# Decay attention and two expert layers on one core: the first head pair's scores from fp32 products of q and k as loaded, and the order list made anew

## The chip, the cores and the metric

The program runs on one core of a Trainium2 chip. The metric is device time in microseconds (us); three runs of the kernel before gave 971.85, 974.48 and 971.40, the median is 971.85.

## What is computed

Attention with a decay over 4 x 8 heads of 576 positions and 64 columns, then two layers, each an expansion to 2048 columns, an elementwise function and a contraction to 512, over 2304 tokens.

```python
scores = scale * np.matmul(q, k.transpose(0, 1, 3, 2))
log_f = np.log(np.clip(f, 0.0001, 1.0))
cum = np.cumsum(log_f, axis=-1)
decay = cum[:, :, :, None] - cum[:, :, None, :]
scores = np.where(causal, -1000000000.0, scores + decay)
attn = np.exp(scores - np.max(scores, axis=-1, keepdims=True))
attn = attn / (np.sum(attn, axis=-1, keepdims=True) + 1e-09)
out = np.matmul(attn, v)
```

The row term of the decay drops out with the row maximum, so only the column term, -8 times the running sum of log f, is added to the unscaled scores.

## The kernel before

**Attention.** The 32 heads are 16 pairs; the two heads of a pair lie in partitions 0 to 63 and 64 to 127. A pair has nine score blocks (S0 to S8): the last 64 rows of both heads together (576 columns, cut into 320 and 256, through q with the other head's half zeroed, `qd`), and for each of four further row blocks one block a head, of 512, 384, 256 and 128 columns. The two heads of such a row block are products on the two row halves of the array. A score is the sum of three fp32r products of high and low parts: `hi` (ScalarE, L415) casts k and q to the high part, `lo` (L419, VectorE or GpSimd) subtracts, `diag` (L422) makes qdh and qdl. Per block, in `tasks_of_pair`: S on TensorE (L460, L469), M the sum with the decay and mask and its row minimum on VectorE (L509), E the exponential on ScalarE (L521), T the transposes on TensorE (L533), C their copy out of PSUM on ScalarE or VectorE (L381, L383); per pair the value products V (L570, fp32 on column halves), the copy O of their sum, and R1 to R6 for the row sums.

**The decay.** f is loaded into 32 partitions (`ft`), clipped (L655), its logarithm taken (L706) and summed along the row by a scan (L658). From pair 1 on a pair's decay comes back from DRAM, broadcast over the partitions (`cb`, stored by L712, loaded by L227 and L230), and GpSimd masks it (L238). The first pair does not wait for that way: the sums are split into a high and a low part (L665, L671), four DMAs carry these rows to partitions 0, 1, 64 and 65 of `ct` (L233), and a fourth product with ones (`one`, `oned`) adds them into the scores.

**The layers.** `gemm_in` (h, L758) and `gemm_out` (a, L852, L854; in the filling time L839) are again three products of parts each. Two of the five token chunks of layer 1 go, for four of 16 weight groups, between the attention's products. Weights come as 64-bit floats and are taken apart by ScalarE, VectorE and GpSimd (`convert`, `split`).

**The order.** All is written by hand as tasks with an engine, a duration, dependences and buffers; `plan` goes through them like a list scheduler and writes each engine's instructions in the order of its own clock. `NUDGE` moves the keys of given tasks. Each engine runs its list in order and waits where an operand isn't there. TensorE begins with 26 warming products on zeros (`warm`, L652).

Of the kernel before, what the change touches and what calls it, by code (L numbers as in the profile page):

```python
# [7 lines left out]
F32 = mybir.dt.float32  # L8
# [10 lines left out]
def kernel(ctx, tc, qT, kT, v, f, w_in1, w_out1, w_in2, w_out2, a, b, out):  # L19
# [21 lines left out]
    W_EARLY = 4  # L41
    W_MID = 5
# [99 lines left out]
    def w_load(m, g, half):  # L142
# [43 lines left out]
    for n in range(2):  # L191
        POOL.memset(vt[n][0:QB, NC - 1, :], 0.0)
        POOL.memset(rt_[n][:], 0.0)
    one, oned = [ap1.tile([P, P], F32R, name=f"one{x}") for x in range(2)]
    half = ap1.tile([P, 2], F32, name="half")
    POOL.memset(half[:], 0.0)
    POOL.memset(oned[:].bitcast(F32), 0.0)
    for j in range(2):
        pp = slice(j * QB, (j + 1) * QB)
        POOL.memset(half[pp, j:j + 1], 1.0)  # L200
        POOL.memset(oned[j * QB:j * QB + 2, pp].bitcast(F32), 1.0)
    POOL.memset(one[:].bitcast(F32), 1.0)
    POOL.memset(ct[0][:].bitcast(F32), 0.0)
# [20 lines left out]
    def load_c(pr):  # L224
        if pr:
            t = cb[pr % 2]
            SP.dma_start(t[:, 0:2, :].rearrange("p j s -> p (j s)"), cd[pr:pr + 1, :].broadcast_to([P, 2 * S]))  # L227
        for j in range(2):
            if pr:
                SP.dma_start(t[j * QB:(j + 1) * QB, 2, :], cd[pr:pr + 1, j * S:(j + 1) * S].broadcast_to([QB, S]))  # L230
                continue
            for x in range(2):
                SP.dma_start(ct[0][j * QB + x:j * QB + x + 1, :].bitcast(F32), ft[j:j + 1, 2 + x, :].bitcast(F32))  # L233
# [38 lines left out]
    MOVE, LAND = 1.4, 1.4  # L272
# [118 lines left out]
    def tasks_of_pair(pr):  # L391
# [777 lines left out]
```

## Time and profile before

| what | us |
|---|---|
| median of three runs | 971.85 |
| span of the profiled execution | 969.2 |
| TensorE busy | 956.1 (99%) |
| VectorE busy | 707.6 (73%) |
| ScalarE busy | 629.7 (65%) |
| GpSimd busy | 436.0 (45%) |

For the profiled execution the page gives the span from the first to the last instruction, and no other time. TensorE's products are pipelined, so a busy share of 99% says that something was under way, and not that it ran at its peak. The attention takes about the first 215 us, the first layer lasts to about 570, the second to the end. PEld is the loading of weights into the array, SPq the issuing of DMAs by SyncE.

### The profile page before, as it was taken

How to read it: one execution, taken by the hardware profiler on the slowest of the kernel's cores; microseconds unless marked ns; L12 is line 12 of the kernel's file. 1: busy time of each engine (PE TensorE's matmuls, PEld its weight loads, DVE VectorE, ACT ScalarE, POOL GpSimd, SP SyncE). 2: the span in 40 equal slices, each digit the busy share in tenths (PEclk: the TensorE clock that was granted, in tenths of full speed). 3: DMA queues.
4: the chain of work that ended last, by engine and by line, in shares of the span. 5: the costliest groups of instructions: out<-in, count | busy, mean ns of one | idle time of the engine just before them, and what ended most of it. 6: DMA issues, size and time to landing. Idle time of an engine off the chain costs nothing.

```text
span 969.2 us, 15465 instructions
## 1 busy us (share of the span) xinstructions
PE 956.1 (99%) x5124; PEld 783.1 (81%) x5124; DVE 707.6 (73%) x1391; ACT 629.7 (65%) x1327; POOL 436.0 (45%) x490
## 2 busy tenths in 40 slices
PE   8999999999999999999999999999999999999998
PEld 5667777778888888888888998888888888888887
DVE  7898889963878967867755779776666766766565
ACT  6999888875654434334334579777677677766675
POOL 3766745636455422322221235444445454444444
PEclk9999999999999999999999999999999999999999
DMA  7897798756553565755742650010101100010010
GB/s 231 256 287 236 230 284 283 246 174 197 189 192 110 163 209 161 238 174 158 244 131 88 196 168 7 1 44 0 44 12 33 44 1 23 0 44 1 1 44 23
DMA packets 66656, 125.14 MB, mean 129 GB/s; under 512 B 10048, under 2 KB 20944, under 8 KB 66576
## 3 DMA queue, kind: packets, MB, share of 16 engines
q1 hardware_dynamic: 66576, 124.16, 40.0%
q8 instruction: 40, 0.66, 0.3%
q14 instruction: 40, 0.33, 0.1%
HBM read 94.61 MB, written 29.51 MB: 128 GB/s over the span
## 4 chain that ended last, share of the span: by engine, by line
PE 80%; DVE 2%; ACT 1%; issue 0%; POOL 0%; ACTq 0%
PE h L758 38%; PE a L854 20%; PE a L852 17%; PE T L533 1%; PE O L570 1%; PE a L839 1%; PE S L469 1%; DVE wd L113 1%; DVE wd L107 0%; DVE wd L101 0%; PE S L460 0%; ACT wh L127 0%; ACT t L782 0%; DVE t L786 0%; POOL wl L131 0%
## 5 line engine op out<-in xcount | busy, mean ns | idle before, releaser
L772 POOL TENSOR_TENSOR gl<-t,gh 128x512 fp32r<-128x512 f32 (+1 forms) x160 | 196.3, 1228 | 278.7 <-ACT gh L768 202.2
L758 PE MATMUL h<-xh,wl 128*128 128x512 f32 (+1 forms) x640 | 236.9, 370 | 0.2 <-POOL wl L131 0.2
L758 PE MATMUL h<-xl,wh 128*128 128x512 f32 (+1 forms) x640 | 235.5, 368 | 0.0
L758 PE MATMUL h<-xh,wh 128*128 128x512 f32 (+1 forms) x640 | 235.5, 368 | 0.0
L768 ACT CAST gh<-t 128x512 fp32r<-128x512 f32 (+1 forms) x160 | 93.0, 582 | 117.1 <-PE a L854 47.2
L803 POOL TENSOR_TENSOR t<-t,t 128x512 f32<-128x512 f32 (+1 forms) x80 | 94.5, 1181 | 129.5 <-ACT t L796 121.2
L758 PEld LDWEIGHTS h<-xh,wl 128*128 128x128 f32 x640 | 120.6, 188 | 20.9 <-POOL wl L131 0.6
L758 PEld LDWEIGHTS h<-xh,wh 128*128 128x128 f32 x640 | 120.6, 188 | 20.0
L758 PEld LDWEIGHTS h<-xl,wh 128*128 128x128 f32 x640 | 120.7, 189 | 19.8
L854 PE MATMUL a<-wh,gl 128*128 128x512 f32 x288 | 112.2, 389 | 0.0
L854 PE MATMUL a<-wl,gh 128*128 128x512 f32 x288 | 112.2, 389 | 0.0
L854 PE MATMUL a<-wh,gh 128*128 128x512 f32 x288 | 112.0, 389 | 0.0
L852 PE MATMUL a<-gh,wl 128*128 128x512 f32 (+1 forms) x288 | 105.3, 366 | 0.0
L852 PE MATMUL a<-gl,wh 128*128 128x512 f32 (+1 forms) x288 | 105.3, 365 | 0.0
L852 PE MATMUL a<-gh,wh 128*128 128x512 f32 (+1 forms) x288 | 105.2, 365 | 0.0
L782 ACT ACTIVATE t<-t 128x512 f32<-128x512 f32 (+1 forms) x80 | 47.1, 589 | 75.8 <-DVE t L777 75.6
L777 DVE TENSOR_SCALAR t<-h 128x512 f32<-128x512 f32 (+1 forms) x80 | 50.8, 635 | 60.2 <-PE h L758 59.7
L821 DVE SCALAR_TENSOR_TENSOR t<-t,na,h 128x512 f32<-128x512 f32 (+1 forms) x80 | 55.3, 691 | 53.3 <-ACT h L817 52.4
L521 ACT ACTIVATE P<-P,nm 128x384 f32<-128x384 f32 (+3 forms) x144 | 84.1, 586 | 15.6 <-DVE nm L509 14.6
L807 DVE TENSOR_TENSOR t<-h,t 128x512 f32<-128x512 f32 (+1 forms) x80 | 51.0, 637 | 55.4 <-ACT t L799 55.1
L238 POOL TENSOR_SCALAR_AFFINE_SELECT cb<-cb 128x128 f32<-128x128 f32 (+1 forms) x150 | 56.2, 387 | 62.9 <-DVE nm L509 47.4
L793 ACT ACTIVATE t<-h,ab 128x512 f32<-128x512 f32 (+1 forms) x80 | 51.8, 649 | 43.5 <-PE h L758 43.5
(121 smaller groups left out, 1883.6 us busy)
## 6 DMA issues: line engine op xcount, KB each, us to landing
raw<-in_moe_w_in_dram SPq DMA_DIRECT2D x32, 512.0 KB, 3.7
raw<-in_moe_w_out_dram SPq DMA_DIRECT2D x32, 512.0 KB, 4.2
xr<-xd SPq DMA_DIRECT2D x48, 256.0 KB, 3.9
wfd<-wd SPq DMA_DIRECT2D x42, 256.0 KB, 4.2
wf<-wfd SPq DMA_DIRECT2D x42, 256.0 KB, 2.6
cb<-cd SPq DMA_DIRECT2D x15, 576.0 KB, 9.4
ks<-in_k_dram SPq DMA_DIRECT2D x16, 288.0 KB, 4.7
qs<-in_q_dram SPq DMA_DIRECT2D x16, 288.0 KB, 4.7
```

What stands on the lines that cost most here:

```text
L238: POOL.affine_select(out=t, in_=t, compare_op=ALU.is_ge, fill=-BIG, base=0, pattern=[[-1, n]], channel_multiplier=1,)
L521: ACT.activation(p, p, AF.Exp, scale=-1.0, bias=nm[pr][:, pos:pos + 1], accum_out=ls[pr][:, COL[pos]:COL[pos] + 1])
L758: PE.matmul(hps[g], ww[:, kk * P:(kk + 1) * P], xx[kk], start=(kk == 0 and y == 0), stop=(kk == KD - 1 and y == 2))
L768: ACT.copy(gt[g][0], mid[g][0])
L772: eng.tensor_tensor(out=lo, in0=mid.pop(g)[0], in1=hi.bitcast(F32), op=ALU.subtract)
L777: DVE.tensor_scalar(out=c, in0=hps[g], scalar1=-1.0, scalar2=1.0, op0=ALU.max, op1=ALU.min)
L793: ACT.activation(mid[g]["w"], hps[g], AF.Abs, scale=ab[:, 0:1])
L803: POOL.tensor_tensor(out=vv, in0=vv, in1=mid[g]["w"], op=ALU.add)
L807: DVE.tensor_tensor(out=t, in0=hps[g], in1=t, op=ALU.mult)
L821: DVE.scalar_tensor_tensor(out=t, in0=t, scalar=na[:, 0:1], in1=hps[g], op0=ALU.add, op1=ALU.mult)
L852: PE.matmul(acc[x, d], ww[:, dd], gg, start=st, stop=sp)
L854: PE.matmul(acc[x, d], gg[:, dd], ww[:], start=st, stop=sp)
```

## The change

1. *First pair's scores.* k and q are used as loaded, in plain fp32 (`whole`): one product a block, with `qdw` for the last rows. hi, lo and the two diag of this pair go.
2. *Its decay.* f is loaded twice, into partitions 0 to 31 and 64 to 95 of `fr` (the tile `cb[0]`); the rest is set to 1. The scan runs over all 128 partitions, and a product with a selector (`sel`, `seld`: -8 in the row of a head, zero elsewhere) adds that head's running sum to the scores. The split, the four DMAs, ct, one and oned go.
3. *The opening.* k and q of the first pair are loaded from ScalarE's queue ahead of its table load; GpSimd's fills come in another order; k and q of the second pair are loaded behind the store of the decay. 9 warming products instead of 26.
4. *The order list.* Durations and latencies of the planner are set anew, and NUDGE holds 57 other moves.

The core of the diff (the list of nudges is left out but for a line):

```diff
-    WARM, WARM2 = 12, 14
+    WARM, WARM2 = 9, 0
...
+    qdw = [ap1.tile([P, P], F32, name=f"qdw{n}") for n in range(2)]
...
-    one, oned = [ap1.tile([P, P], F32R, name=f"one{x}") for x in range(2)]
...
+    sel, seld = [ap1.tile([P, P], F32, name=f"sel{x}") for x in range(2)]
...
     def load_pair(pr, x):
...
-            SP.dma_start(t[:], (kT, qT)[x][pr])
+            (SP if pr else ACT).dma_start(t[:], (kT, qT)[x][pr])
...
     def load_c(pr):
...
-            for x in range(2):
-                SP.dma_start(ct[0][j * QB + x:j * QB + x + 1, :].bitcast(F32), ft[j:j + 1, 2 + x, :].bitcast(F32))
...
     NUDGE = [
-        (648, 29, -0.8), (1339, 23, 1.6), (1564, 5, 0.5), (1173, 66, -1.2), (4043, 36, 0.6), (240, 8, -16.0),
...
+        (390, 54, -1.7), (1376, 60, 5.4), (263, 28, 0.9), (453, 2, 3.3), (1491, 27, -3.5), (882, 18, -2.1),
...
         def diag(y, eng):
+            to, src = (qdw[pr % 2], nat[pr, 1]) if whole else ((qdh, qh), (qdl, ql_))[y]
+            src = src[:, S - QB:S]
             ENGINES[eng].tensor_tensor(
-                out=(qdh, qdl)[y][:].rearrange("p (x s) -> p x s", x=2),
-                in0=(qh, ql_)[y][:, S - QB:S].bitcast(F32).unsqueeze(1).to_broadcast([P, 2, QB]),
+                out=to[:].rearrange("p (x s) -> p x s", x=2),
+                in0=(src if whole else src.bitcast(F32)).unsqueeze(1).to_broadcast([P, 2, QB]),
...
-            T("ldc", -99, "sp", [(0.55, 0.05)] * 4, lambda: load_c(pr), ((0, "c"),), ("cb",))
+            T("ldc", -99, "init", 0.0, lambda: None, (), ("cb",))
         ways = ["dvp", "pool"]
         lo_ = [0.68, 1.42]
-        for x, (nm_, tag) in enumerate((("k", "ks"), ("q", "qs"))):
+        if whole:
+            T("qd0", kk + 3, ways, [0.24, 0.4], [lambda e=e: diag(0, e) for e in ways], ("ldq",), ("qdw",))
...
             def s_fn(s=s, b=b, both=both, cuts=cuts):
+                if whole:
+                    k_, q_, cum = nat[pr, 0], nat[pr, 1], fr[:, 1, :]
...
-                        ways = [(qdl[:], kh[:, n0:n1]), (qdh[:], kl_[:, n0:n1]), (qdh[:], kh[:, n0:n1])]
-                        if pr == 0:
-                            ways.append((oned[0:QB + 2], c_[0:QB + 2, n0:n1]))
+                        if whole:
+                            ways = [(qdw[pr % 2][:], k_[:, n0:n1])] + ([] if pr else [(seld[:], cum[:, n0:n1])])
+                        else:
+                            ways = [(qdl[:], kh[:, n0:n1]), (qdh[:], kl_[:, n0:n1]), (qdh[:], kh[:, n0:n1])]
...
-                for x, (qq, kk_) in enumerate(((ql_, kh), (qh, kl_), (qh, kh)) + (((one, c_),) if pr == 0 else ())):
+                if whole:
+                    ways = [(q_[:, qc], k_)] + ([] if pr else [(sel[:], cum)])
+                else:
+                    ways = [(ql_[:, qc], kh), (qh[:, qc], kl_), (qh[:, qc], kh)]
+                for x, (qq, kk_) in enumerate(ways):
                     for jj in range(2):
                         pp = slice(jj * QB, (jj + 1) * QB)
-                        PE.matmul(
-                            ts[jj][:, 0:n], qq[pp, qc] if x < 3 else qq[pp, :], kk_[pp, 0:n], start=(x == 0),
-                            stop=(x == (2 if pr else 3)),
-                        )
+                        PE.matmul(ts[jj][:, 0:n], qq[pp, :], kk_[pp, 0:n], start=(x == 0), stop=(x == len(ways) - 1))
...
-    ft = ap1.tile([NH, 4, S], F32R, tag="PT1", name="ft")
-    zt = ap1.tile([NH, S], F32, tag="PT0", name="zt")
-    SP.dma_start(ft[:, 0, :].bitcast(F32), f.rearrange("b h s -> (b h) s"))
+    fr = cb[0]
+    zt = ap1.tile([P, 1], F32, name="zt")
+    f_ = f.rearrange("b h s -> (b h) s")
+    SP.dma_start(fr[0:NH, 0, :], f_)
+    SP.dma_start(fr[QB:QB + NH, 0, :], f_)
+    load_pair(0, 0)
+    load_pair(0, 1)
+    ACT.preload_act_table_set("natural_log_exp_and_others")
     still = ap1.tile([P, 512], mybir.dt.bfloat16, tag="P", name="still", bufs=PB)
     DVE.memset(still[:], 0.0)
     DVE.memset(zt[:], 0.0)
-    load_pair(0, 0)
-    load_pair(0, 1)
+    DVE.memset(fr[NH:QB, 0, :], 1.0)
+    POOL.memset(fr[QB + NH:P, 0, :], 1.0)
+    POOL.memset(half[:], 0.0)
+    for j in range(2):
+        POOL.memset(half[j * QB:(j + 1) * QB, j:j + 1], 1.0)
+
+    def equal(t, base):
+
+        n = t.shape[1]
+        POOL.affine_select(
+            out=t, in_=t, compare_op=ALU.not_equal, fill=-ROOT, base=base, pattern=[[0, n]], channel_multiplier=1,
+        )
+
+    for t in (seld, sel):
+        POOL.memset(t[:], 0.0)
+        for j in range(2):
+            pp = slice(j * QB, (j + 1) * QB)
+            equal(t[pp, pp if t is seld else slice(0, P)], -j)
...
-    cum = ft[:, 1, :].bitcast(F32)
-
-    def c_hi():
-        ACT.activation(ft[:, 2, :], cum, AF.Copy, scale=-ROOT)
+    cum = fr[:, 1, :]
 
     def c_all():
-        ACT.activation(ft[:, 0, :].bitcast(F32), cum, AF.Copy, scale=-ROOT)
-
-    def c_lo():
-        DVE.scalar_tensor_tensor(
-            out=ft[:, 3, :], in0=cum, scalar=-ROOT, in1=ft[:, 2, :].bitcast(F32), op0=ALU.mult, op1=ALU.subtract
-        )
+        ACT.activation(fr[0:NH, 2, :], cum[0:NH, :], AF.Copy, scale=-ROOT)
...
-    t = task(-99, "act", 0.57, c_hi, (t,))
-    t2 = task(-98, "act", 0.57, c_all, (t,))
-    t = tid[0, "c"] = task(-99, "dve", 0.67, c_lo, (t,))
+    t = tid[0, "c"] = task(-99, "dve", 1.35, lambda x=x: f_scan(cum, x), (t,))
+    t = task(-99, "act", 0.57, c_all, (t,))
```

**TensorE, the first pair's scores, before** (S are score tiles, kh and kl the parts of k, ql, qh, qdl, qdh those of q, ct the decay's rows):

```order
L652 LDWEIGHTS still
L652 MATMUL warm<-still 128x512
L460 MATMUL S_0_224<-kh_115,qdl_124 128x320 [waits DVE_49,Activation_49]
L460 MATMUL S_0_224<-kl_116,qdh_123 128x320
L460 MATMUL S_0_224<-kh_115,qdh_123 128x320
L460 MATMUL S_0_224<-ct_129,one_139 128x320 [waits DMAHW2_49,DMAHW1_49,DMAHW3_49,DMAHW0_49,Pool_49]
L460 MATMUL S_320_229<-kh_115,qdl_124 128x256
L460 MATMUL S_320_229<-kl_116,qdh_123 128x256
L460 MATMUL S_320_229<-kh_115,qdh_123 128x256
L460 MATMUL S_320_229<-ct_129,one_139 128x256
L469 MATMUL S_0_236<-kh_115,ql_120 128x512
```

**and with the change** (ks, qs are k and q as loaded, qdw q with the other half zeroed, cb the tile of the running sums, sel the selectors):

```order
L661 LDWEIGHTS still
L661 MATMUL warm<-still 128x512
L433 MATMUL S_0_191<-ks_129,qdw_111 128x320 [waits DMAHW0_49,Pool_49]
L433 MATMUL S_0_191<-cb_113,sel_123 128x320 [waits DVE_49]
L433 MATMUL S_320_194<-ks_129,qdw_111 128x256
L433 MATMUL S_320_194<-cb_113,sel_123 128x256
L446 MATMUL S_0_202<-ks_129,qs_131 128x512 [waits DMAHW2_49]
L446 MATMUL S_0_203<-ks_129,qs_131 128x512
L446 MATMUL S_0_202<-cb_113,sel_122 128x512
L446 MATMUL S_0_203<-cb_113,sel_122 128x512
```

Three products of parts and one with the rows that DMAs bring have become one of k and q and one with the running sums; the first now waits for a DMA and for GpSimd, the second for VectorE.

**ScalarE, from the logarithm of f to the first exponentials, before** (P are the exponentials' tiles, nm the row minima):

```order
L706 ACTIVATE ft<-ft 32x576 [waits DVE_49]
L665 ACTIVATE ft<-ft 32x576 [waits DVE_49]
L668 ACTIVATE ft<-ft 32x576 [waits Activation_49]
L415 CAST kh_115<-ks_157 128x576 [waits DMAHW1_49]
L415 CAST qh_119<-qs_159 128x576 [waits DMAHW2_49]
L415 CAST kh_117<-ks_179 128x576 [waits DMAHW5_49]
L415 CAST qh_121<-qs_182 128x576 [waits DMAHW6_49]
L521 ACTIVATE P_250,ls_249<-P_250,nm_248 128x576 [waits DVE_49]
L521 ACTIVATE P_257,ls_249<-P_257,nm_248 128x512 [waits DVE_49]
L521 ACTIVATE P_272,ls_249<-P_272,nm_248 128x512 [waits DVE_49]
```

**and with the change**:

```order
L181 DMA ks_129<-in_k_dram 128x576
L181 DMA qs_131<-in_q_dram 128x576
L621 ACT_TABLE_LOAD
L708 ACTIVATE cb_113<-cb_113 128x576 [waits DMAHW3_49,DMAHW1_49,DVE_49]
L674 ACTIVATE cb_113<-cb_113 32x576 [waits DVE_49]
L496 ACTIVATE P_212,ls_211<-P_212,nm_210 128x576 [waits DVE_49]
L380 CAST kh_101<-ks_198 128x576 [waits DMAHW7_49]
L496 ACTIVATE P_225,ls_211<-P_225,nm_210 128x512 [waits DVE_49]
L496 ACTIVATE P_228,ls_211<-P_228,nm_210 128x512 [waits DVE_49]
L346 COPY PT_1_254<-T_0_238 128x8x64 [waits PE_49]
```

The casts of the second pair (kh_117, qh_121 before, kh_101, qh_105 now) have moved from ahead of the first exponential to behind the first and the fourth, and one copy of transposes stands between.

**GpSimd, the end of its fills, with the change** (tri are the masks of the first pair, vt and rt tiles for v and the row sums):

```order
L643 MEMSET tri 128x512 [waits Pool_49]
L644 MEMSET tri_120 128x256
L199 AFFINE_SELECT tri<-tri 128x128 [waits Pool_49]
L199 AFFINE_SELECT tri_120<-tri_120 64x64 [waits Pool_49] x2
L648 MEMSET ident 128x128 [waits Pool_49]
L649 AFFINE_SELECT ident<-ident 128x128 [waits Pool_49]
L654 MEMSET vt_115 64x128
L655 MEMSET rt_117 128x128
L654 MEMSET vt_116 64x128
L655 MEMSET rt_118 128x128
L389 TENSOR_TENSOR qdw_111<-qs_131,half 128x128 [waits DMAHW2_49]
L199 AFFINE_SELECT cb_114<-cb_114 64x64 [waits DMAHW4_49]
```

The last instruction that the first product waits for, qdw, stands behind all fills and ahead of the first mask of pair 1; before, GpSimd had no part in q here, and its fills were followed by that mask at once.

## Rows read from the trace of the kernel before

**Rows 1.** Stretches: length, busy us by engine, granted clock, DMA share, GB/s.

```profile
20.00:40.00 20.00, 19.08 (x158) 13.16 (x156) 18.37 (x63) 19.82 (x63) 13.13 (x23) 1.00 0.83 256
...
300.00:400.00 100.00, 99.79 (x441) 82.33 (x440) 81.44 (x123) 42.00 (x70) 35.08 (x25) 1.00 0.54 169
```

**Rows 2.** Timeline, opening: start, length, engine, line, operation; in brackets idle before.

```profile
2.70 0.45 DVE L655 TENSOR_SCALAR ft<-ft 32x576 f32<-32x576 f32 x1 [0.90 <-DMA ft<-in_f_dram]
...
3.27 0.58 SPq L215 DMA_DIRECT2D ks<-in_k_dram  x1
...
3.90 1.35 DVE L658 TENSOR_TENSOR_SCAN ft<-ft,zt 32x576 f32<-32x576 f32 x1 [0.75 <-ACT ft L706]
...
7.00 2.48 SPq L233 DMA_DIRECT2D ct<-ft  x4
```

**Rows 3.** The same timeline, TensorE.

```profile
1.26 7.56 PE L652 MATMUL warm<-still 128*128 128x512 bf16 x26 [1.26 <-DVE still L643]
...
9.10 0.39 PE L460 MATMUL S<-kh,qdl 128*128 128x320 f32 x1 [0.28 <-ACT qh L415]
...
10.78 0.39 PE L460 MATMUL S<-ct,one 66*128 66x320 f32 x1 [1.00 <-DMA ct<-ft]
```

**Rows 4.** Stretches of 1 us; PEclk is the granted clock.

```profile
11.00:12.00 1.00, 1.00 (x7) 0.83 (x8) 0.32 (x1) 0.00 (x0) 0.00 (x0) 0.86 0.87 255
12.00:13.00 1.00, 1.00 (x8) 0.74 (x6) 0.67 (x4) 0.26 (x1) 0.00 (x0) 0.50 0.73 270
...
15.00:16.00 1.00, 1.00 (x11) 0.83 (x12) 0.82 (x3) 1.00 (x5) 0.00 (x0) 0.94 0.83 212
```

**Rows 5.** Who waited for whom, TensorE, whole run: us, times, longest.

```profile
PE T L533 <- ACT PT L381: 3.2, 6, 0.9
...
PE h L758 <- POOL wl L131: 0.2, 1, 0.2
```

**Rows 6.** The same view, TensorE's weight loads, 20 to 215 us.

```profile
PEld S L469 <- issue: 4.4, 26, 0.2
PEld O L570 <- issue: 3.5, 17, 0.3
...
PEld T L533 <- issue: 2.2, 11, 0.3
```

**Rows 7.** Timeline, GpSimd, opening and one product with half.

```profile
2.25 0.53 POOL L172 TENSOR_SCALAR_AFFINE_SELECT tri<-tri 64x64 f32<-64x64 f32 x2
...
3.71 0.20 POOL L197 MEMSET one<- 128x128 f32 x1
...
4.29 0.34 POOL L201 MEMSET one<- 2x64 f32 x2
...
4.68 0.58 POOL L203 MEMSET ct<- 128x576 f32 x1
...
26.32 0.40 POOL L422 TENSOR_TENSOR qdl<-ql,half 128x128 fp32r<-128x128 f32 x1
```

**Rows 8.** DMA issues of the whole run: KB each, median us to landing.

```profile
ks<-in_k_dram SPq DMA_DIRECT2D x16, 288.0 KB, 4.7
```

**Rows 9.** The chain that ended last: start, length, line, instructions.

```profile
212.29 2.86 PE O L570 x28
...
278.09 2.72 PE h L758 x12
```

**Rows 10.** Timeline, TensorE, row pairs of 512 columns and the next.

```profile
20.80 0.40 PE L469 MATMUL S<-kh,qh 64*128 64x512 f32 x2
...
21.03 0.59 PE L469 MATMUL S<-kh,ql 64*128 64x384 f32 x2
```

**Rows 11.** Timeline, ScalarE, casts and the first exponentials.

```profile
7.66 0.67 ACT L415 CAST kh<-ks 128x576 fp32r<-128x576 f32 x1
...
12.74 0.77 ACT L521 ACTIVATE P<-P,nm 128x576 f32<-128x576 f32 x1 [3.70 <-DVE nm L509]
...
14.31 0.72 ACT L521 ACTIVATE P<-P,nm 128x512 f32<-128x512 f32 x1 [0.70 <-DVE nm L509]
```

More of the change, by code (lines that the diff above doesn't have):

```diff
@@ L41 @@
     W_EARLY = 4
+    WHOLE = 1
     W_MID = 5
@@ L438, in tasks_of_pair @@
               (nm_ + "hi",), (), (tag,))
-        T("qd0", kk + 3, ways, [0.24, 0.4], [lambda e=e: diag(0, e) for e in ways], ("qhi",))
-        T("qd1", kk + 3, ways, [0.24, 0.4], [lambda e=e: diag(1, e) for e in ways], ("qlo",))
+        if not whole:
+            T("qd0", kk + 3, ways, [0.24, 0.4], [lambda e=e: diag(0, e) for e in ways], ("qhi",))
+            T("qd1", kk + 3, ways, [0.24, 0.4], [lambda e=e: diag(1, e) for e in ways], ("qlo",))
         for pos, (b, j) in enumerate(BLOCKS):
@@ L478, in tasks_of_pair @@
             else:
-                np_ = 3 if pr else 4
-                dur = np_ * sum(mm(n1 - n0) for n0, n1 in cuts) if both else np_ * max(mm(w), 0.12)
-                T(f"S{pos}", s, "pe", 0.02 + dur, s_fn, ("klo", "qlo", "qd0", "qd1", prev) + (() if pr else ("ldc",)), ("S", "S"),
-                  ("k", "q") if pos == NB - 2 else ())
+                np_ = 3 if not whole else 4 if pr else 8
+                dur = np_ * sum(mm(n1 - n0) for n0, n1 in cuts) + 0.05 if both else np_ * max(mm(w), 0.11 if whole else 0.095) - 0.01
+                deps = ("ldk", "ldq", "qd0", prev) + (() if pr else ("c",)) if whole else ("klo", "qlo", "qd0", "qd1", prev)
+                free = (("qdw",) if whole and both else ()) + ((("ks", "qs") if whole else ("k", "q")) if pos == NB - 2 else ())
+                T(f"S{pos}", s, "pe", 0.02 + dur, s_fn, deps, ("S", "S"), free)
                 if not both:
@@ L494, in tasks_of_pair @@
             if pr:
-                T(f"K{pos}", s + KM - KMK, "pool", 0.55 if both else 0.33, mask_fn, ("ldc",) if pos < 3 else (f"M{pos - 2}",))
+                T(f"K{pos}", s + KM - KMK, "pool", 0.6 if both else 0.27, mask_fn, ("ldc",) if pos < 3 else (f"M{pos - 2}",))
             def max_fn(s=s, w=w, pos=pos, both=both, j=j):
@@ L621, in tasks_of_pair @@
         kr = s0 + NB - 1 + KR
-        T("R1", kr, "dvp", 0.25, r1, [f"E{p}" for p in range(NB)])
+        T("R1", kr, "dvp", 0.34, r1, [f"E{p}" for p in range(NB)])
         T("R2", kr + 1, "pe", 0.2, r2, ("R1",), ("T",))
@@ L644 @@
     DVE.memset(zt[:], 0.0)
-    load_pair(0, 0)
-    load_pair(0, 1)
+    DVE.memset(fr[NH:QB, 0, :], 1.0)
[13 more added lines that the diff above has]
+            equal(t[pp, pp if t is seld else slice(0, P)], -j)
+    POOL.memset(tri[:], 0.0)
+    POOL.memset(tri2[:], 0.0)
+    no_later(tri[:, 384:512])
+    for j in range(2):
+        no_later(tri2[j * QB:(j + 1) * QB, 192:256])
+    POOL.memset(ident[:], 1.0)
+    POOL.affine_select(
+        out=ident[:], in_=ident[:], compare_op=ALU.is_equal, fill=0.0, base=0,
+        pattern=[[-1, P]], channel_multiplier=1,
+    )
+    for n in range(2):
+        POOL.memset(vt[n][0:QB, NC - 1, :], 0.0)
+        POOL.memset(rt_[n][:], 0.0)
     def warm(n):
@@ L956 @@
             for part in range(3):
-                t = task(key, "pe", mm(n, W_EARLY), lambda x=x, k=k, part=part: gemm_out1(x, early, k, part),
+                t = task(key, "pe", mm(n, W_EARLY) + 0.03, lambda x=x, k=k, part=part: gemm_out1(x, early, k, part),
                          deps if t is None else (t,), ("O",) if t is None else (), ("g",) * W_EARLY if k == KD - 1 and part == 2 else ())
```

73 lines of the change are left out of this document (21 added, 52 removed), and 14 rows, old and new, of the table NUDGE.

## Prediction

> **What bounds the kernel now.** I first read the busy time by stretch. From 20 us on TensorE is busy nearly all the time: 19.08 of 20 us early, 99.79 of 100 later [rows 1], so behind the opening a microsecond saved on TensorE is a microsecond of the end. But in 20 to 40 us ScalarE is busy 19.82 of 20 [rows 1]: there two engines are full, and TensorE's lead can be lost to ScalarE.
>
> Second, the opening in order of time. The decay takes a long way: f is clipped at 2.70, scanned from 3.90 for 1.35, and then split, and its rows are carried by four small DMAs issued from 7.00 [rows 2]. TensorE shows what ends last: 26 warming products until 8.82, the first real product at 9.10, and a stop of 1.00 us for those DMAs before the decay product at 10.78 [rows 3]. The clock pays for the stops: the granted clock is 0.86 in 11 to 12 us, 0.50 after it and 0.94 in 15 to 16 [rows 4], so from about 11.7 to 15.1 the engine ran at 1.2 instead of 2.4 GHz.
>
> Third, the waits in 20 to 215 us, where the order list decides. TensorE waits 3.2 us in all for ScalarE's copies of transposes [rows 5], and its weight loader shows 26 stops of 4.4 us before row pairs, 17 of 3.5 before value products and 11 of 2.2 before transposes that nothing releases [rows 6]: they stand where the array changes between whole, row halves and column halves, 10.1 us over 54, 0.19 us each.
>
> **The change, part by part.** The sum runs against this execution. Only its span is shown, 969.2 us; the median of the three runs is 971.85, so 2.65 us lie around it, and I keep that constant and add every saving to 971.85.
>
> *Start of the first product: -2.6 us.* Two things must be ready, beside q and k. The selector of the last block is now made by GpSimd behind all its fills, as the order shows. Before, GpSimd's fills end at 5.26, and each of their kinds has its row [rows 7]. Gone are two "one" fills (0.20 each), two small ones (0.34 together) and ct (0.58): 1.3. New are one fill of a quarter of ct's partitions with as many columns (0.58), two of 0.20 and four selects at 0.27: 2.0. So it is free at about 6.0, the selector takes 0.40 [rows 7], and with the handing over the product starts at 6.5 instead of 9.10. Shortest: 6.0, if the new pieces overlap; longest: 7.1, if every piece waits for the one before. q and k are now issued from ScalarE's queue, beside f instead of behind it; one issue (about 0.5) behind the start at 0.8, the median landing of 4.7 us [rows 8] gives 6.0: covered.
>
> *The stop of 1.00 us goes: -1.0.* The second load of f is issued one issue later (0.58 at most in [rows 2]), so the clip starts at 3.3, and the scan, whose end stands 2.55 behind the clip's start in [rows 2], ends at 5.85. The decay rows are then where TensorE reads them: no split, no DMA. The cover is the selector on GpSimd, 0.65 us later; even a second f landing that much late costs nothing.
>
> *More work on TensorE: +3.2.* An fp32 product is dearer. The value products are the row for it: 28 records, 14 products, 1600 columns of paired halves, 2.86 us [rows 9], that is 1.79 ns a column for a pair of halves. Two row halves of the present kind run side by side (two of 512 columns, and the next two start 0.23 us later, [rows 10]), and so I read the value products' halves too; then a whole-array product costs the same 1.79 ns. New: scores and decay, 2 x 1856 columns (576 + 512 + 384 + 256 + 128) = 6.6 us. Old: four rounds at 0.45 ns a column [rows 10], 4 x 0.84 = 3.4. Were the value products' halves run one after the other, the last block's 576 columns would cost half, and the term +2.2; the upper end is +3.7, with the small blocks at twice their columns. The Trainium skill, page FP8 and Floating Point Precision, section TensorE Precision Notes, says that true fp32 makes four passes through the array; by it the new products alone would be an estimated 6.2 us at 2.4 GHz, and the sum 0.4 us lower; it speaks against the half-price reading.
>
> *The clock: 0.* Warming is cut from 26 to 9 products. Before, 26 take 7.56 us [rows 3], and the first ones ran at half the pace of the last; 9 slow ones (0.43 us, 512 columns at 1.2 GHz) end at 5.1, and TensorE then has nothing for 1.4 us. In the trace two stops, 0.28 and 1.00 us, stand before a fall of 3.4 us [rows 3, 4]. The one stop ahead is longer, so I take one fall of the same length at the same price, 1.7 us of lost work in both. Ends: -1.7 if it doesn't fall, +1.0 if it is low from the first product on.
>
> *What moves into the busy stretch.* Pair 1's casts and subtractions, in the idle opening until now (from 7.66 on, [rows 11]), now stand between the first pair's exponentials: two casts of 0.67 on ScalarE [rows 11], two subtractions and two small products on VectorE. In exchange the exponential of block 0 starts near 9.6 instead of 12.74 and, with S1 at the low clock, the second near 12.6 instead of 14.31 [rows 11]. ScalarE's lead of 1.7 to 3.1 pays for them and little is left: 0 to 1 us at 20 us. The new list takes 11 copies of transposes away from ScalarE and gives them to VectorE (99 to 88, 45 to 56), which keeps ScalarE from holding TensorE. I book 0.
>
> *Fewer changes of the array: -1.7.* Counted over the whole order, TensorE changes between whole, rows and columns 110 times now, 101 after: 9 x 0.19 [rows 6]. Ends: 0, if each such stop then becomes a wait for ScalarE, and -2.
>
> *Other waits of the new list: 0*, from -2 (most of the 3.2 us of [rows 5]) to +3 (as much again).
>
> *The rest.* The matmuls behind the attention are the same number, TensorE stays full there, and the last 48 are the same; their changed sequence I book at 0. The casts and subtractions of pair 0 that go lay in the idle opening: 0.
>
> Sum: -2.6 - 1.0 + 3.2 + 0 - 1.7 = -2.1, so 969.7 us (968.0 to 971.4 with the small ends).
>
> **The rivals.**
> *The clock holds* through the first pair. For it: one stop instead of two, and dense products behind. Against: a fall stands right behind such stops in [rows 3, 4]. It gives 969.7 - 1.7 = 968.0. [...]
> *The new list waits less.* If 2.2 of the 3.2 us of waits for ScalarE's copies go [rows 5], with ScalarE's 11 copies less: 967.5. Against: VectorE has them now, and was busy 18.37 of the same 20 us [rows 1].
> *Pair 1's k is late.* SyncE now issues it behind the store of the decay, which waits for ScalarE's copy, at about 7.0 instead of 3.27 [rows 2]. ScalarE's cast of it stands ahead of the second exponential, so a late k holds every exponential behind it. At the median landing, 4.7 us [rows 8], the cast is ready at 11.7, before 12.6: nothing. It decides from a landing of 5.0 us; at 9.3, twice the median, the second exponential is 3.7 us late and the end 973.4. Against: nothing but v is on the queues by then.
> *The new list starves TensorE behind the attention.* This is the one that ends slower. By the order, the first product of the expert layer runs up to 11 groups ahead of the second there; before, 4. It stands on 4 PSUM buffers, 5 of t1 and 3 of g: 12. If the weights of two groups come one group late, TensorE stands twice for 2.72 us [rows 9]: 969.7 + 5.4 = 975.1. It decides from the second late group on. For it: the only wait there now is for a weight split, 0.2 us [rows 5], so they come just in time. Against: TensorE waited nowhere else there.
>
> **How the numbers follow.** A measurement of this kernel can tell about 0.3%, 2.9 us, from no change. Forecast 0.50, of which 0.12 below 968.9; clock holds 0.15; fewer waits 0.15; late k 0.10 (+1.6, within); starved 0.10. Faster 0.12 + 0.15 + 0.15 = 0.42, same 0.38 + 0.10 = 0.48, slower 0.10. The range takes in the clock together with fewer waits (969.7 - 1.7 - 2.2 = 965.8) and most of the late k: 965.8 to 972.9.
>
> **What would show it.** Right: the first product at 6.0 to 7.1, released by GpSimd; no stop before the decay product; 6.6 us of products in the first pair at full clock; one fall of the granted clock before 13 us; about 10 us of stops at changes become 8.5. Wrong: a first product below 6, a clock that stays at 1.00, a cast of pair 1's k that waits for a DMA, or more than 1 us of TensorE waits behind 215 us.

## The result, and the profile after

The changed kernel takes 984.97 us (median of four runs, 984.17 to 985.85) against 971.85: ratio 1.0134 [1.0119, 1.0150], slower by 13.1 us, where 969.7 was forecast. The profiled execution spans 983.7 us, before 969.2.

Stretches of the kernel after (length, busy us of TensorE, its weight loads, VectorE, ScalarE, GpSimd, then the granted clock, DMA share, GB/s), the counterpart of [rows 1, 4]:

```profile
7.00:8.00 1.00, 0.22 (x1) 0.22 (x2) 0.54 (x1) 0.43 (x1) 0.73 (x1) 0.76 0.00 0
8.00:9.00 1.00, 1.00 (x2) 0.62 (x3) 0.00 (x0) 0.25 (x1) 0.00 (x0) 0.50 0.00 0
9.00:10.00 1.00, 1.00 (x3) 0.68 (x2) 0.00 (x0) 0.00 (x0) 0.00 (x0) 0.50 0.65 118
10.00:11.00 1.00, 1.00 (x4) 0.74 (x3) 0.00 (x0) 0.00 (x0) 0.00 (x0) 0.53 0.90 281
11.00:12.00 1.00, 1.00 (x6) 0.43 (x6) 0.31 (x1) 0.00 (x0) 0.00 (x0) 1.00 0.97 353
...
20.00:40.00 20.00, 19.11 (x161) 13.50 (x161) 18.17 (x63) 19.55 (x60) 10.60 (x23) 1.00 0.75 235
40.00:60.00 20.00, 17.37 (x140) 12.13 (x141) 18.61 (x62) 18.11 (x56) 14.04 (x21) 1.00 0.79 241
60.00:100.00 40.00, 36.35 (x256) 26.98 (x252) 34.12 (x103) 33.26 (x92) 24.75 (x44) 0.91 0.85 264
100.00:150.00 50.00, 46.59 (x343) 35.92 (x344) 43.19 (x126) 38.78 (x108) 24.56 (x50) 0.97 0.83 247
150.00:215.00 65.00, 61.59 (x470) 46.09 (x471) 58.29 (x171) 54.47 (x155) 31.78 (x62) 1.00 0.79 244
...
300.00:400.00 100.00, 97.81 (x429) 80.08 (x428) 72.01 (x111) 40.86 (x67) 35.58 (x27) 1.00 0.47 150
```

The same stretches of the kernel before:

```profile
40.00:60.00 20.00, 19.38 (x158) 13.43 (x157) 17.93 (x58) 18.71 (x59) 15.64 (x27) 1.00 0.89 288
60.00:100.00 40.00, 36.69 (x266) 26.93 (x268) 35.37 (x106) 35.88 (x103) 24.11 (x45) 1.00 0.77 235
100.00:150.00 50.00, 49.64 (x379) 38.14 (x375) 43.22 (x132) 44.40 (x125) 27.99 (x49) 1.00 0.84 265
150.00:215.00 65.00, 63.68 (x504) 48.65 (x502) 55.94 (x169) 55.61 (x159) 35.07 (x64) 1.00 0.74 237
```

The loss isn't in the opening and not in 20 to 40 us, where TensorE is as busy as in [rows 1]. It lies behind: TensorE is busy 2.0 us less in 40 to 60 us, 3.1 less in 100 to 150, 2.1 less in 150 to 215 and 2.0 less in 300 to 400, and in 60 to 150 us its clock is lower.

The opening in order of time, kernel after (start, length, engine, line, operation; idle before), beside [rows 2, 3, 10, 11]:

```profile
0.80 0.42 ACTq L181 DMA_DIRECT2D ks<-in_k_dram  x1
...
4.97 0.46 DVE L664 TENSOR_SCALAR cb<-cb 128x576 f32<-128x576 f32 x1 [3.06 <-POOL tri L199]
...
6.18 1.36 DVE L667 TENSOR_TENSOR_SCAN cb<-cb,zt 128x576 f32<-128x576 f32 x1 [0.75 <-ACT cb L708]
6.71 1.02 POOL L389 TENSOR_TENSOR qdw<-qs,half 128x128 f32<-128x128 f32 x1
...
7.78 1.44 PE L433 MATMUL S<-ks,qdw 128*128 128x320 f32 x2 [3.02 <-POOL qdw L389]
...
9.01 1.27 PE L433 MATMUL S<-cb,sel 128*128 128x320 f32 x2
...
11.46 1.13 PE L446 MATMUL S<-ks,qs 64*128 64x512 f32 x4
...
12.75 0.78 ACT L496 ACTIVATE P<-P,nm 128x576 f32<-128x576 f32 x1 [4.50 <-DVE nm L484]
```

The clip starts at 4.97 (forecast 3.3), the first product at 7.78 (forecast 6.5), the first exponential at 12.75, where it was 12.74: the opening wins nothing, and at 20 us the kernel is some 0.5 us late (pair 1's second mask product starts at 21.09, before at 20.56).

Who waited for whom, kernel after: TensorE over the whole run ([rows 5]); then GpSimd and VectorE in 20 to 215 us.

```profile
PE T L508 <- DVE PT L348: 5.3, 6, 2.3
PE T L508 <- ACT PT L346: 4.0, 9, 0.8
PE S L433 <- POOL qdw L389: 3.0, 1, 3.0
...
PE a L852 <- DVE t L865: 1.4, 2, 0.8
...
PE h L758 <- POOL wl L125: 0.8, 1, 0.8
...
POOL xa L594 <- DMA R<-rcd: 20.9, 11, 4.0
POOL cb L199 <- DMA cb<-cd: 15.5, 11, 4.0
...
DVE P L484 <- POOL cb L199: 9.3, 12, 2.1
```

The same view of its weight loads, 20 to 215 us, beside [rows 6]:

```profile
PEld S L446 <- issue: 5.2, 28, 0.3
PEld O L545 <- issue: 4.3, 18, 0.4
PEld T L508 <- issue: 4.0, 10, 2.2
```

Against that, GpSimd and VectorE in the same stretch of the kernel before:

```profile
POOL xa L619 <- DMA R<-rcd: 4.6, 2, 3.7
...
DVE P L509 <- POOL cb L238: 1.0, 2, 0.8
```

GpSimd now stands for transfers of R and cb, and VectorE for GpSimd's masks. That looked like the cause; but the kernel is no faster without these waits (e3).

### The profile page after: what moved, and what is told of

The parts are those of the page before. It is cut to its first block, busy times and chain, and to the rows that moved or that the text cites. A ratio compares the mean times of both kernels' runs of the same rounds, so it can differ in the third digit from the quotient of the medians.

```text
span 983.7 us, 15428 instructions
## 1 busy us (share of the span) xinstructions
PE 958.9 (97%) x5107; PEld 783.5 (80%) x5107; DVE 712.9 (72%) x1403; ACT 627.1 (64%) x1310; POOL 429.6 (44%) x491
## 4 chain that ended last, share of the span: by engine, by line
PE 78%; DMA 6%; DVE 5%; issue 3%; ACT 2%; POOL 1%; SPq 1%; POOLq 0%; ACTq 0%; DVEq 0%
PE h L758 35%; PE a L854 20%; PE a L852 16%; PE T L508 2%; PE O L545 2%; DMA cb<-cd 1%; PE a L839 1%; DMA R<-rcd 1%; PE S L446 1%; DMA wfd<-wd 1%; DMA raw<-in_moe_w_in_dram 1%; DVE P L484 1%; DMA raw<-in_moe_w_out_dram 1%; DVE wd L107 1%; DVE wd L101 1%
## 5 line engine op out<-in xcount | busy, mean ns | idle before, releaser
L496 ACT ACTIVATE P<-P,nm 128x384 f32<-128x384 f32 (+3 forms) x144 | 83.9, 584 | 21.8 <-DVE nm L484 21.3
L199 POOL TENSOR_SCALAR_AFFINE_SELECT cb<-cb 128x128 f32<-128x128 f32 (+1 forms) x150 | 52.5, 367 | 57.1 <-DVE nm L484 29.1
L508 PE MATMUL T<-ident,P 128*128 128x128 f32 x400 | 66.6, 289 | 10.9 <-DVE PT L348 5.3
```

Source lines behind the costliest of these rows:

```text
L199: POOL.affine_select(out=t, in_=t, compare_op=ALU.is_ge, fill=-BIG, base=0, pattern=[[-1, n]], channel_multiplier=1,)
L496: ACT.activation(p, p, AF.Exp, scale=-1.0, bias=nm[pr][:, pos:pos + 1], accum_out=ls[pr][:, COL[pos]:COL[pos] + 1])
L508: PE.transpose(ps[:, (c - c0) * P:(c - c0 + 1) * P], p[:, k0:k0 + P], ident[:])
```

## The experiments

The kernel before ran beside each group: 971.0 to 971.9 us. "Idle" is the length of the stretch less TensorE's busy time, in one profiled execution; the clock is the granted clock in 20 to 215 us.

| run | opening | list | us | ratio | idle 20-215 | idle 215-400 | clock |
|---|---|---|---|---|---|---|---|
| before | before | before | 971.85 | | 6.5 | 0.2 | 1.00 |
| after | changed | changed | 984.97 | 1.0134 [1.0119, 1.0150] | 14.0 | 2.2 | 0.97 |
| e1 | changed | before | 974.60 | 1.0034 [1.0022, 1.0047] | 9.0 | 0.2 | 1.00 |
| e2 | before | changed | 983.13 | 1.0126 [1.0111, 1.0141] | 16.8 | 1.9 | 1.00 |
| e3 | changed | changed, landings back | 987.29 | 1.0169 [1.0149, 1.0190] | 9.5 | 4.7 | 0.99 |
| e4 | changed | changed, no shifts | 983.26 | 1.0128 [1.0083, 1.0172] | 13.6 | 0.0 | 0.96 |
| e5 | before | before, no shifts | 978.92 | 1.0076 [1.0061, 1.0091] | 8.3 | 0.6 | 0.97 |
| e6 | changed | old durations, no shifts | 985.31 | 1.0141 [1.0126, 1.0156] | 9.2 | 1.6 | 0.98 |
| e18 | changed | old durations, old shifts | 983.72 | 1.0121 [1.0106, 1.0137] | 10.4 | 1.2 | 0.99 |
| e7 | mended | before | 976.56 | 1.0046 [1.0032, 1.0061] | 9.4 | 1.9 | 0.99 |
| e8 | mended, ScalarE | before | 972.91 | 1.0013 [1.0003, 1.0023] | 8.2 | 1.2 | 0.99 |
| e9 | e8, 3 buffers | before | 971.87 | 1.0004 [0.9994, 1.0013] | 7.1 | 1.7 | 1.00 |
| e10 | e7, 3 buffers | before | 971.33 | 0.9998 [0.9989, 1.0007] | 6.7 | 1.2 | 1.00 |
| e11 | changed, 3 buffers | changed | 981.04 | 1.0097 [1.0082, 1.0112] | 11.2 | 1.0 | 0.99 |
| e12 | changed | changed, xa later | 998.45 | 1.0284 [1.0267, 1.0301] | 21.3 | 1.2 | 0.96 |
| e13 | e10, wl on VectorE | before | 970.33 | 0.9984 [0.9974, 0.9994] | 6.7 | 0.5 | 1.00 |
| e17 | e9, wl on VectorE | before | 970.55 | 0.9994 [0.9985, 1.0003] | 6.8 | 0.3 | 1.00 |

### Opening and list apart: e1, e2

The planner's result was replaced by a list written out: in e1 the changed kernel with every later task in before's order, in e2 the reverse.

```diff
     def plan(first, wk):
-        ...
+        return [(int(t) // 4, tasks[int(t) // 4][1][int(t) % 4][2]) for t in FIXED[first > 0].split()]
```

> The changed opening (first pair in fp32, decay by selector, fills, loads, warming as changed) with every later instruction in the order of the kernel before. List theory (the new order list costs the 13 us): 971 to 974 us, with the opening alone some 0.5 us late. Opening theory (the moved conversions and the dearer products cost it, through the later stages): 982 to 986.

> The opening of the kernel before (parts, four DMAs, 26 warming products) with every later instruction in the order of the changed kernel. List theory: 982 to 986 us. Opening theory: 970 to 974.

The list alone costs 983.13 - 971.22 = 11.9 us, the opening alone 3.4; together they cost 13.1. So the opening is no gain even in the old order, and most of the loss is the list's.

### What the list is made from: e3 to e6, e18

```diff
-    MOVE, LAND = 1.1, 1.3
+    MOVE, LAND = 1.4, 1.4
```

That is e3. e4 has `NUDGE = []` in the changed kernel, e5 in the kernel before; e6 is e4 with all of before's durations, lags and landings; e18 is e6 with before's 30 shifts at the same tasks (their numbers less 8).

> The changed kernel with only the planner's two DMA constants set back (MOVE and LAND 1.4 and 1.4 instead of 1.1 and 1.3), nudges kept; the list is planned anew. If the list is bad because it counts on landings that are too early: 972 to 978 us. If it is the nudges, that fit only their own list, or the other durations: 981 or more.

> The changed kernel with no nudges, all its durations and DMA constants kept. If the too early landings do the harm: 981 or more, since they stand in this list too. If the nudges do: 972 to 979.

> The kernel before with its table of 30 shifts emptied; durations and opening are its own. Theory A (before's shifts are what made its list good, and the change threw them away with the old numbering, so that its own 57 shifts are no match): about as slow as the changed kernel, 980 to 986 us. Theory B (the new durations in the table are what spoils the list, the shifts are worth little): within 3 us of before, 970 to 975.

> The changed kernel with all durations, lags and the two DMA constants of before put back and no shifts; only the opening's own tasks differ from the kernel before without shifts. Theory A (shifts): as slow as the changed kernel and as before without shifts, 980 to 986 us, since the list has no shifts either. Theory B (durations): the list is good again and the opening's +3.4 us is left, 973 to 977 us. Either way it should stand about 3 us above the run of before without shifts.

> As the old durations without shifts (985.31 us), with before's 30 shifts at the same tasks. Theory A (the shifts are worth their 7.4 us wherever the list is much the same): 975 to 979 us. Theory N (a shift fits one list only: the opening's tasks alone change 415 of 4491 rows of TensorE's order, so before's shifts meet another list): 981 to 987.

GpSimd's waits of e3, 20 to 215 us:

```profile
POOL cb L199 <- DMA cb<-cd: 3.5, 1, 3.5
...
POOL xa L594 <- DMA R<-rcd: 2.0, 2, 1.7
```

With the old landings the waits of the changed kernel for R and cb are gone (20.9 to 2.0, 15.5 to 3.5), TensorE's idle time in the attention falls from 14.0 to 9.5, and the kernel is no faster: now the layers stand for 4.7 us. So the planner's shorter landings make those waits, and those waits don't make the time. Putting the old durations back doesn't help either: with them and no shifts the kernel takes 985.31, with the new ones and no shifts 983.26. The shifts have a price: before's own list without its 30 shifts takes 978.92, so they were worth 7.4 us. That the changed kernel's 57 are worth anything on the chip isn't shown (984.97 with them; without, the two executions took 979.6 and 986.9). And the old shifts don't carry over: in e18 only the opening's tasks differ from before in what the list is made from, but between the lists without shifts (e5 and e6) that alone changes 415 of the 4491 rows of TensorE's order that were compared, and the old shifts bring 1.6 of their 7.4 us, with overlapping intervals.

### The opening mended: e7, e8

Both have before's order behind the opening. In e7 k and q are issued on SP behind f, GpSimd makes qdw ahead of its late fills, and 11 warming products run; in e8 ScalarE makes qdw.

```diff
-    WARM, WARM2 = 9, 0
+    WARM, WARM2 = 11, 0
...
-            (SP if pr else ACT).dma_start(t[:], (kT, qT)[x][pr])
+            SP.dma_start(t[:], (kT, qT)[x][pr])
...
-            T("qd0", kk + 3, ways, [0.24, 0.4], [lambda e=e: diag(0, e) for e in ways], ("ldq",), ("qdw",))
+            T("qd0", kk + 3, ways, [0.24, 0.4], [lambda e=e: (diag(0, e), late_fills()) for e in ways], ("ldq",), ("qdw",))
```

> Every later instruction in before's order, the changed opening (fp32 products, selector product), but k and q of pair 0 are issued on SP behind f, and GpSimd fills tri, ident, vt and rt only behind qdw; 11 warming products. Theory C (the opening came late because f shared its landing with k and q issued beside it, and qdw stood behind fills and ran beside the scan): clip at 3.2 to 3.6 us in place of 4.88, qdw ends by 6.3 in place of 7.65, first product at 5.5 to 6.5, and 970 to 972 us, 2.5 to 4 below the 974.6 of the changed opening with the old list. Rival D (f lands late for another reason, or the slow-clocked fp32 products set the end of the opening anyway): the time stays at 973.5 to 975.

> As the mended opening, but qdw is made by ScalarE in two activations of 64 columns with a per-partition scale, and GpSimd does not touch it. Theory C: like the mended opening on GpSimd or up to 0.5 us lower, since ScalarE is idle between the Ln and the conversion of the scan: 969.5 to 972 us. Rival D: 973.5 to 975. If GpSimd's 1.02 us beside the scan matters, the first product starts 0.4 to 0.8 us earlier here than in the mended opening; if q's landing sets it, at the same time.

The opening of e7 in order of time:

```profile
3.33 0.46 DVE L673 TENSOR_SCALAR cb<-cb 128x576 f32<-128x576 f32 x1 [1.42 <-DMA cb<-in_f_dram]
...
4.54 1.36 DVE L676 TENSOR_TENSOR_SCAN cb<-cb,zt 128x576 f32<-128x576 f32 x1 [0.75 <-ACT cb L717]
...
5.54 0.55 POOL L397 TENSOR_TENSOR qdw<-qs,half 128x128 f32<-128x128 f32 x1 [1.60 <-DMA qs<-in_q_dram]
...
6.14 0.81 PE L441 MATMUL S<-ks,qdw 128*128 128x320 f32 x2 [0.70 <-POOL qdw L397]
...
8.28 1.13 PE L454 MATMUL S<-ks,qs 64*128 64x512 f32 x4
...
11.06 0.78 ACT L504 ACTIVATE P<-P,nm 128x576 f32<-128x576 f32 x1 [2.17 <-DVE nm L492]
```

Theory C holds for the opening itself: f, issued at 0.8 and 1.25 us as in the changed kernel, is clipped at 3.33 instead of 4.97 once k and q come behind it. (After the change the profile names GpSimd's tri fill as the end of the clip's wait; in e4, with the same opening, f is seen to land 3.7 us behind an issue at 1.26, and the clip follows at 5.06.) The first product stands at 6.14, the granted clock is 1.00 in each stretch from 6 to 10 us, and the first exponential starts 1.7 us earlier than before. And the whole kernel is no faster than e1: 976.56, with overlapping intervals. A gain that TensorE has at 11 us isn't there at 60. e8, where ScalarE does the same work, has its first product at 6.31 and not earlier, so in both it is q's landing, at about 5.5, that sets it. Yet e8 takes 3.7 us less than e7: the end hangs on something behind the opening.

### Three buffers for raw k and q: e9, e10, e11

What SP waits for in 8 to 20 us, e7:

```profile
SPq L181 <- PE S L454: 4.5, 1, 4.5
```

The same of the kernel before:

```profile
SPq L215 <- DVE nm L509: 0.7, 3, 0.3
```

Before, the conversions let go of pair 0's raw k and q. The fp32 products read them until the pair's last score product, so the load of pair 2's k waits 4.5 us, and everything queued on SP behind it, the decay of the next pairs among it, waits too. VectorE then stands 3.1 us for a mask before pair 2 (e7), and e7, 2.1 us ahead of before at pair 1's second mask product, is 2.9 behind from pair 5 on. In e1 the same wait is 6.3 us, and the kernel is 1.1 us behind before at pair 1 and 3.9 at pair 2: the wait is probably most of the 3.4 us that the changed opening costs. A third buffer takes the wait's reason away:

```diff
-            t = ap2.tile([P, S], F32, tag=("ks", "qs")[x], name=f"{'kq'[x]}s{pr}")
+            t = ap2.tile([P, S], F32, tag=("ks", "qs")[x], name=f"{'kq'[x]}s{pr}", bufs=3)
```

> As qdw on ScalarE, every instruction in the same order, but the raw k and q have three buffers in place of two. Theory E (the fp32 products read pair 0's raw k and q until its last score product, so SP's load of pair 2's k stands 4.6 us behind them, and all that is queued on SP behind it, the decay loads of the next pairs first, is late; before, the conversions let go of the buffers earlier): SP's wait for a score product goes, VectorE's wait of 2.7 us at 27 to 30 us for the mask shrinks, TensorE is busy 38 us or more of 20 to 60 (37.1 now), 969 to 971 us. Rival G (the old order just doesn't fit another opening, whatever holds it): 972 to 975 us, the stop moves elsewhere.

> The same third buffer for the mended opening with qdw on GpSimd (976.6 us with two). Theory E: 3 to 6 us less, 970 to 973, close to the ScalarE one. Rival G: within 1.5 us of 976.6 or unrelated to it.

> The changed kernel with its own list, and three buffers for raw k and q in place of two; the list is made with the old count, so no instruction moves. Theory E for the changed kernel as well: 3 to 6 us less, 979 to 982. Theory F (its loss is made in the whole attention, by the list): the wait for pair 2's load comes once, so 983.5 to 985.5, no change.

Theory E holds for the mended opening: e10 takes 5.2 us less than e7, in 8 to 20 us SP's longest wait is 1.8, and the lead of 1.4 us at pair 1 is still 1.1 at the last pair. The changed kernel itself gains 3.9 (e11), in its own list, but not where theory E puts it. It has no wait of SP for a score product in 8 to 20 us; its waits for a load of k there are

```profile
SPq L181 <- DVE kl L384: 1.9, 1, 1.9
```

and some shorter ones. Up to pair 5 the second mask products of e11 start within 0.9 us of those of the changed kernel; e11 is ahead from pair 6 on but for pair 9, at the last pair by 6.1. What the buffer frees there stays open. For e9 the times alone can't tell it from e8 (971.87 and 972.91, overlapping intervals), and TensorE's 37.60 busy us in 20 to 60 miss the 38 expected; VectorE's wait for the mask there went from 3.1 to 0.2. Behind a third buffer, too, the changed kernel stays 9.7 us above the mended opening with before's list (e11, e10).

### Moving parts of the list: e12, e14 to e16

> The changed kernel's own list, but the GpSimd product xa and the store behind it stand some 30 tasks (about 4 us) later in it, 16 times; nothing else moves. Theory F (GpSimd reaches xa before its DMA has landed, 20.9 us of waiting in 20 to 215, and the masks behind it and SP's store come late with it): the wait of xa falls under 8 us, VectorE's wait for masks (8.6 us) to under 4, and the time falls by 4 to 8 us, 977 to 981. Rival H (these waits would only be filled with others, the list loses elsewhere): 983.5 to 986.

GpSimd's waits of e12, 20 to 215 us:

```profile
POOL cb L199 <- DMA cb<-cd: 21.2, 11, 9.0
...
POOL xa L602 <- DMA R<-rcd: 2.0, 2, 1.2
```

Theory F falls. The wait of xa went as meant, 20.9 to 2.0 us, and the kernel lost 13.5 more: masks now wait 21.2 us for cb (15.5 without the move), and TensorE's idle time rises to 21.3. The store behind xa moved along on SP; which loads it held up there was not followed.

The last attempt put GpSimd's order (e14), SP's (e15) or both (e16) of before's attention under the changed list of the other engines, with three buffers. In e14 and e16 pair 9's decay comes into its buffer before pair 7 has read it to the end, so a part of pair 7's scores is made with pair 9's decay; the work is the same.

> The changed kernel's list with three buffers (981.04 us), but GpSimd's instructions of the attention stand in before's order; all other engines and SP keep the new order. Theory K (the masks and xa stand badly on GpSimd): 3 to 8 us less, 973 to 978. Theory L (SP's order of loads and stores is it) or M (the order of the computing engines is it): 979.5 to 983.

> The same, but SP's loads and stores of the attention stand in before's order (three of them excepted, which the other orders don't allow) and GpSimd keeps the new one. Theory L: 3 to 8 us less, 973 to 978, with the masks' wait for cb (25.9 us) mostly gone. Theories K and M: 979.5 to 983.

> Both SP's and GpSimd's order from before under TensorE's, ScalarE's and VectorE's new order. Theories K or L: as the better of the two single ones or 1 to 3 us below it, 971 to 976. Theory M (the new order of TensorE, VectorE and ScalarE itself, with work of two pairs interleaved otherwise, loses): 979 to 985, nothing gained by either queue.

1045.85, 1040.63 and 1021.77 us: all theories missed. In e15 TensorE is idle for 39.6 us of 20 to 215 at a clock of 0.86. Here the old order of one queue under the new list of the others was a large loss each time, so it can't tell which rows of the new list carry its loss; that stays open.

### Where the opening's lead goes: e13, e17

In e10 the attention's last pair is 1.1 us ahead of before (its second mask product starts at 195.81, before at 196.94), and the end isn't. TensorE waits 1.2 us for GpSimd's `wl`, at 310 and 320 us. VectorE's part of the weights there, e10, with the GpSimd products beside it and behind it:

```profile
306.75 1.40 POOL L781 TENSOR_TENSOR gl<-t,gh 128x512 fp32r<-128x512 f32 x1 [0.76 <-ACT gh L777]
...
307.03 1.67 DVE L107 SCALAR_TENSOR_TENSOR wd<-raw,wd 128x512 int32<-128x512 int32 x1
...
309.43 1.34 POOL L125 TENSOR_TENSOR wl<-wd,wh 128x512 fp32r<-128x512 f32 x1 [1.28 <-ACT wh L121]
```

The same instructions in the kernel before, where these lines stand six further down (its L113 is L107 in e10):

```profile
307.08 0.69 DVE L107 SCALAR_TENSOR_TENSOR wd<-raw,wd 128x512 int32<-128x512 int32 x1
...
307.52 1.41 POOL L772 TENSOR_TENSOR gl<-t,gh 128x512 fp32r<-128x512 f32 x1 [0.76 <-ACT gh L768]
...
307.81 1.67 DVE L113 SCALAR_TENSOR_TENSOR wd<-raw,wd 128x512 int32<-128x512 int32 x1
...
310.22 1.35 POOL L131 TENSOR_TENSOR wl<-wd,wh 128x512 fp32r<-128x512 f32 x1 [1.29 <-ACT wh L127]
```

So the shift behind gl takes 1.67 us in both kernels, and the slowing that theory J below counts on is nothing new in e10. What differs is small: in e10 the weights come 0.8 us earlier than before, and TensorE, more than that ahead, has to wait for them.

```diff
         def s1(eng=POOL):
+            eng = DVE if m == 0 and g >= 12 else eng
```

> As the GpSimd opening with three buffers (971.33 us), but the last eight wl differences of the first layer's weights run on VectorE instead of GpSimd. Theory J (the opening's lead of 1.1 us at the end of attention is given back because TensorE then waits for wl at 310 and 320 us, GpSimd's product taking 1.3 us and slowing VectorE's shifts beside it from 0.69 to 1.66): the wait h<-wl goes from 1.2 us to under 0.3 and the time is 969.8 to 970.5 us, 1 below before. Rival (the weights' loads set it): stays at 971 to 971.6 us, the wait is the same or names VectorE.

> The ScalarE opening with three buffers (971.87 us, attention ends 0.5 us earlier than with GpSimd's) and the last eight wl of the first layer on VectorE. If the weights' wait was what gave the lead back: 969.3 to 970.3 us, at or below the 970.33 of e13. Rival (the run to run spread hides it, or another wait comes): 970.3 to 971.5.

Theory J holds in part. With wl on VectorE, 0.69 us instead of 1.34, the wait for it goes from 1.2 to 0.5, not below 0.3, and e13 takes 970.33 us, ratio 0.9984 [0.9974, 0.9994]: the best of all here, 1.5 us under the kernel before, still inside the 0.3% of no change, and its interval overlaps that of e10. The ScalarE opening (e17) adds nothing to it.

## Why the prediction was wrong

*Other waits of the new list: 0, from -2 to +3.* This step failed, and with it the forecast. The list costs 11.9 us (e2). I read the waits of the old list and assumed that another list by the same planner would have about the same; e5 shows that the old list had been better than its planner by 7.4 us, through 30 shifts, and a new list starts without that. With the changed list in before's opening (e2) TensorE is idle for 16.8 us of 20 to 215, before for 6.5. The bound of +3 should have been the price of a list without fitting shifts, and no row of before shows that price; it takes a run.

*Start of the first product: -2.6.* It came at 7.78, not 6.5: -1.3. Two sizes were wrong. GpSimd's fills ended at 6.7, not 6.0. And the selector was priced at 0.40 on GpSimd as if it ran alone; beside the scan it took 1.02. The scan stood there because f was late: it was taken to land one issue later for its second part, 3.3; with k and q beside it from the other queue it was clipped at 4.97, without them at 3.33 (e7).

*The stop of 1.00 goes: -1.0.* Right: no stop stands before the decay product at 9.01.

*More work on TensorE: +3.2.* Right in its price. At full clock (e7) the last block's two products and their decay, 2 x 576 columns, take 8.28 - 6.14 = 2.14 us; by 1.79 ns a column it is 2.06.

*The clock: 0.* It came so in the traced execution, by luck: 0.76, 0.50, 0.50, 0.53 from 7 to 11 us, then 1.00, a fall as long as the one in [rows 4]. With the same opening, nine warming products, other executions differ (e1, then e3):

```profile
7.70 1.44 PE L441 MATMUL S<-ks,qdw 128*128 128x320 f32 x2 [2.42 <-POOL qdw L397]
...
7.76 0.81 PE L433 MATMUL S<-ks,qdw 128*128 128x320 f32 x2 [2.49 <-POOL qdw L389]
```

In e1 the products run at half pace, 1.44 us for two as after the change, from the first one to about 13 us (the trace has no record of the clock ahead of its first rise, and the views show 1.00 there); in e3 they start at full pace, and the clock is 0.50 from 9 to 12 us. Before's opening kept its clock in e2 and e5, behind stops of 0.84 and 0.80 us. The Trainium skill, page TensorE: Matmul & The Clock Gate, section Why this matters for your kernels, names long idle gaps between bursts as what brings the clock down; the fall in the stop of 3.02 us agrees, the one behind 1.00 in [rows 3, 4] doesn't.

*What moves into the busy stretch: 0.* Its 0 to 1 us at 20 us was 0.5, though not by its path: the exponential of block 0 started at 12.75, not 9.6, since the first product was late and at the low clock the last block's products took 3.7 us (7.78 to 11.46) instead of the 2.1 of e7. What I missed there is what stopped moving out: raw k and q are held until the pair's last product. That cost had no term; it is 5.2 us under before's list (e7, e10). In the changed kernel a third buffer brings 3.9 (e11), by waits that were not found.

*Fewer changes of the array: -1.7.* It didn't come: the three rows of TensorE's weight loads above add to 13.5 us over 56 stops, where [rows 6] had 10.1 over 54.

*The rivals.* The clock didn't hold. The new list waits more, not less, [rows 5] against 5.3 and 4.0 above. Pair 1's k was issued at 8.64, and its cast at 13.53 waits for nothing. (That rival's sum is off: if it decides from a landing of 5.0 us, one of 9.3 makes 4.3 us, not 3.7.) The list that starves TensorE behind the attention comes nearest, with 2.2 us idle in 215 to 400 instead of 0.2, past the 1 us that was to show the forecast wrong, but for another reason (VectorE's t and one wl, 0.8 us at the longest) and at less than half of its 5.4. The other 7.5 us of new idle time, and the low clock of 0.91 and 0.97, lie in the attention, where no rival stood. The low clock isn't needed for the loss: in e2 TensorE runs the same list at 1.00 in 20 to 215 us, is idle for longer, and the kernel takes 983.13.

*What adds up and what stays open.* Of the 11.9 us of the list, 7.4 are what a list without shifts costs in the kernel before (e5); with the same opening the changed list (e2) is another 4.2 above e5, and for these no cause is shown. Behind the changed opening a list with before's durations and no shifts (e6) is 10.7 above before's own (e1). That shifts fitted to the new list would win this back is argued and not shown: none were fitted anew. The third buffer's 3.9 us can't be added to this; e1 and e2 add to 15.3, not 13.1, so such pieces don't simply add. Whether a third buffer would help the kernel before wasn't tried.

## What to carry to other kernels

A schedule that was adjusted on the chip is part of the kernel's speed: forecast a change that makes the list anew against the list without its adjustments, and measure that baseline first. When an operand is used as loaded for longer, ask who waits for its buffer, and what stands behind that wait on an in-order queue. A wait that is named large in the profile is not yet the cause: here two such waits were removed (e3, e12), once without gain and once at a loss.

## What the runs showed of the hardware

*VectorE's scan keeps GpSimd out.* qdw ends 0.19 us behind the end of the scan in all 14 traces in which GpSimd makes it: scan to 7.54, qdw to 7.73 after the change; 5.90 and 6.09 in e7; 6.06 and 6.25 in e10, for spans of 1.02, 0.55 and 0.74 us. The Trainium skill, page SBUF — State Buffer, section SBUF: two separate sides, says that a VectorE instruction with two SBUF inputs and a GpSimd one that reads SBUF take the port pair that they share by turns, each for its whole instruction; these ends agree, and VectorE's shifts fit too: in the kernel before one takes 0.69 us where it starts ahead of GpSimd's gl (307.08 and 307.52), the next 1.67 where it starts behind (307.81), and it ends 0.55 behind gl; the same in e10.

*A second queue doesn't bring the first one's data sooner.* With k and q issued on ScalarE's queue beside f on SP, f was clipped 1.64 us later (4.97) than with all on SP (3.33, e7). In every trace with k and q on ScalarE's queue the clip starts between 4.7 and 5.1, with both parts of f and k and q on SP between 3.3 and 3.4. The Trainium skill, page DMA: Bandwidth & Descriptors, section Issuing engines are not separate DMA queues, says that such transfers run on the same 16 engines and interleave; this agrees.
